# W2 in wider products and smaller pieces, another path for the second norm of two blocks, and a new written-out order in a transformer block on one core

## The chip, the core and the metric

The kernel runs on one core of a Trainium2 chip. The core has a matrix engine (TensorE: PE in the profile, PEld for its weight loads), a vector engine (DVE), an activation engine (ACT), GpSimd (POOL) and SyncE (SP), which here issues nearly all DMAs. The metric is the device time of one execution in microseconds. Three runs of the kernel before gave 1135.32, 1136.92 and 1138.43 us; the median is 1136.92.

## The reference

One block of a transformer with adaptive layer norm, on 2048 tokens of 1024 features in bf16. Attention has 32 heads of 32 features for the queries and a single head for keys and values; the feed-forward part is gated and has 3584 hidden features.

```
mod = silu(c) @ w_mod            # six vectors: sa, ca, ga, sb, cb, gb
h = layernorm(x) * (1 + ca) + sa
q = (h @ wq), 32 heads;  k = h @ wk;  v = h @ wv      # one k and one v for all heads
p = softmax(q k^T / sqrt(32))
x = x + ga * ((p v) @ wo)
h = layernorm(x) * (1 + cb) + sb
x = x + gb * ((silu(h @ w1) * (h @ w3)) @ w2)
```

## The kernel before

**Tiles.** The tokens are split into 8 blocks of 256 (`NB`, `B`), each of two tiles of 128 tokens (`t`). Within a block, attention goes over 8 groups of 4 heads (`f`), each group being a "unit" `u = 8n + f`, and over 8 steps `j` of 256 keys. One step `c` (`s_exp`) is 8 score products of 32 rows, which run four at a time in TensorE's row groups, followed by two exponentials on ACT of 128x1024 each, which are written to one of 10 slots of `U`. There are 512 steps, and so 1024 exponentials. The scores use six PSUM banks (`S` in the profile), everything else the other two (`PB`); after the last exponentials the six are used as well.

**Attention's sums.** The denominators are sums over keys: DVE adds pairs of exponentials (`pairs`, into `PS`), then folds these together (`fold`, and the additions in `av`), and TensorE multiplies what is left by ones (`dens`). `av_mm` multiplies the exponentials by V. `attend` transposes, inverts and multiplies, and writes the result over the queries in `QT`.

**After a block's attention.** `wo(n)` multiplies by WO, adds to `X`, takes the statistics of the second norm (`ln_stats`: two BATCH_NORM_STATS2 and an aggregate on DVE, an addition and a power on POOL) and normalises each tile to `XN` (`ln_norm`). The result must then be transposed into `h2t(n)`. In blocks 1 to 6 each tile is transposed by a DMA (DMA_TRANSPOSE), and DVE scales eight rows of 256 in place. In blocks 0 and 7 TensorE transposes through PSUM, in two halves of the features, each of which needs both tiles; DVE scales on the way out. `ffn1` then goes over 14 slabs of 256 hidden features (W1 and W3, 512 KB each, in three slots), with a tanh on ACT for each. `ffn2` multiplies by W2 in four quarters of 256 output columns: `quarter(n, q)` loads 1.8 MB (`w2_dma`, into one of two slots of `W2S`), and runs 28 products of 256 columns for each of the two tiles into the two halves of one bank; `result` scales by `GBR` and adds to `X`. In the last block the last two quarters' weights go to room in `QT` and `U` that is free by then.

**The start.** Sixteen tiles of x are loaded, normalised (`lnt1`: statistics on DVE; the normalising, `nm`, and the evacuation of the transposed tile, `ev`, on ACT or DVE), transposed on TensorE, and projected to K, V and Q. WQ is loaded in two parts. Its first 256 columns are scaled to `WQ0S` for the first heads; later DVE scales all of WQ in place, in eight instructions by row group, for the remaining query projections. `q_bias` makes the bias of the queries by 48 products of one column for six head groups. `mod_chunk` makes four of the modulation vectors from eight pieces of 1 MB.

**Order.** Every operation is a node of a graph with an engine, an estimated duration, a due time `vt` and a tag. `Placer.run` builds each engine's order from these ahead of time: it takes the node that can start first, and among those within a slack the one with the least `vt` plus an offset from `PLAN`. `PLAN` has one entry for each 8 steps of attention: slacks, flags and offsets by tag and engine. On the chip each engine runs its order strictly, with semaphore waits; an SP wait for a free slot holds every DMA behind it. TensorE's products may be emitted in a form of four 32-column products (`prods`, `cols`, profile "128\*32"), which avoids a switch of the array's mode next to V products but has four times the instructions; `mode_of` chooses this form while the run of such products is under `COLS` and an estimate of instruction traffic (`load`) is under `FULL`.

All engine instructions come out of one helper, so the profile gives line 22 for all of them; they are told apart by the tiles that they write and read.

## Time and profile before

| | |
|---|---|
| median of three runs | 1136.92 us |
| the profiled execution | 1139.48 us, of which the span is 1137.5 us |
| granted TensorE clock, mean | 0.992 |
| chain that ended last | PE 48%, ACT 42%, DVE 6% |
| DMA | 209.64 MB, 184 GB/s over the span |
| first exponential starts / last one ends | 30.8 us / 1038.1 us |

The page's first part gives busy time by engine, and the views of the trace group instructions by form ("out<-in", partitions x elements), list them in order of time, or say what ended an engine's idle time. `W2S` holds W2's slots (and, at the start, tiles of x and pieces of w_mod); `HT` holds the first norm's output and later the hidden features and `TS`; `W` is the W1/W3 slots and before that WQ; `WO` holds small things at the start. The idle time that is put down to "issue" is time in which an engine waited for nothing that the profile shows. The mean duration of a matmul includes its way through the array: the spacing of a run of them is shorter.

### The profile page before, as it was taken

How to read it: one execution, taken by the hardware profiler on the slowest of the kernel's cores; microseconds unless marked ns; L12 is line 12 of the kernel's file. 1: busy time of each engine (PE TensorE's matmuls, PEld its weight loads, DVE VectorE, ACT ScalarE, POOL GpSimd, SP SyncE). 2: the span in 40 equal slices, each digit the busy share in tenths (PEclk: the TensorE clock that was granted, in tenths of full speed). 3: DMA queues.
4: the chain of work that ended last, by engine and by line, in shares of the span. 5: the costliest groups of instructions: out<-in, count | busy, mean ns of one | idle time of the engine just before them, and what ended most of it. 6: DMA issues, size and time to landing. Idle time of an engine off the chain costs nothing.

```text
span 1137.5 us, 37371 instructions
## 1 busy us (share of the span) xinstructions
PE 1102.1 (97%) x16835; PEld 752.4 (66%) x16860; DVE 989.8 (87%) x1617; ACT 1020.1 (90%) x1159; POOL 39.1 (3%) x91
## 2 busy tenths in 40 slices
PE   5999998999899999999999999999999999999998
PEld 4744536766467766777577766776567757776887
DVE  7998999999989989998999899998989899997442
ACT  5999999999999999999999999999989999994110
POOL 5200000000000000000000000000000000000000
PEclk9999989999999999999999999999999999999999
DMA  9320586675756666865596577868686558767993
GB/s 347 104 76 22 166 217 187 193 205 139 168 150 194 190 176 160 240 190 151 137 287 192 151 190 202 227 193 216 142 245 192 156 152 226 210 198 197 239 240 103
DMA packets 381535, 209.64 MB, mean 184 GB/s; under 512 B 17600, under 2 KB 373184, under 8 KB 381376
## 3 DMA queue, kind: packets, MB, share of 16 engines
q1 hardware_dynamic: 380944, 207.11, 65.9%
q8 instruction: 133, 2.18, 0.8%
q14 instruction: 26, 0.21, 0.1%
q10 hardware_dynamic: 432, 0.13, 0.0%
HBM read 199.89 MB, written 4.19 MB: 179 GB/s over the span
## 4 chain that ended last, share of the span: by engine, by line
PE 48%; ACT 42%; DVE 6%; DMA 1%; issue 1%; SPq 1%; POOL 0%; DVEq 0%
ACT U L22 39%; PE PB L22 34%; PE S L22 14%; ACT HT L22 3%; DVE PS L22 2%; DMA W<-in_A_wq_dram 1%; DVE ST L22 1%; SPq L22 1%; DVE X L22 1%; DVE RB L22 0%; DVE QT L22 0%; DVE HT L22 0%; DVE XNB L22 0%; DVE WO L22 0%; DVE MV L22 0%
## 5 line engine op out<-in xcount | busy, mean ns | idle before, releaser
L22 ACT ACTIVATE U<-S 128x1024 bf16<-128x1024 f32 x1024 | 966.6, 1142 | 11.5 <-PE S L22 10.7
L22 DVE TENSOR_TENSOR PS<-U 128x2048 bf16<-128x2048 bf16 x256 | 308.2, 1216 | 12.0 <-ACT U L22 10.1
L22 DVE TENSOR_TENSOR PS<-PS 128x1024 bf16<-128x1024 bf16 (+1 forms) x420 | 282.5, 689 | 2.5
L22 PE MATMUL PB<-QT,W 128*128 128x256 bf16 (+1 forms) x2688 | 228.1, 276 | 0.4 <-DVE HT L22 0.4
L22 PE MATMUL S<-QT,KT 32*128 32x256 bf16 x4096 | 204.7, 274 | 10.1 <-ACT U L22 7.8
L22 PEld LDWEIGHTS PB<-QT,W 128*128 128x128 bf16 (+1 forms) x2688 | 171.2, 98 | 42.0 <-issue 23.6
L22 PE MATMUL PB<-W2S,HT 128*128 128x256 bf16 x1512 | 189.3, 273 | 0.0
L22 PEld LDWEIGHTS PB<-W2S,HT 128*128 128x128 bf16 x1512 | 137.4, 98 | 41.5 <-issue 22.0
L22 PEld LDWEIGHTS S<-QT,KT 32*128 32x128 bf16 x4096 | 60.8, 92 | 139.5 <-ACT U L22 130.9
L22 PE MATMUL PB<-U,V 128*32 128x256 bf16 x4096 | 130.9, 276 | 3.5 <-issue 2.3
L22 PEld LDWEIGHTS PB<-U,V 128*32 128x32 bf16 x4096 | 101.8, 97 | 27.8 <-issue 15.3
L22 PE MATMUL PB<-QT,HT 128*128 128x256 bf16 (+1 forms) x1216 | 117.0, 273 | 0.0
L22 PE MATMUL PB<-HT,W 128*32 128x512 bf16 (+2 forms) x884 | 99.2, 343 | 3.1 <-DVE XNB L22 1.0
L22 PEld LDWEIGHTS PB<-QT,HT 128*128 128x128 bf16 (+1 forms) x1216 | 86.4, 97 | 21.0 <-issue 11.4
L22 ACT ACTIVATE HT<-PB 128x512 bf16<-128x512 f32 (+1 forms) x105 | 77.0, 733 | 7.9 <-PE PB L22 7.8
L22 DVE SCALAR_TENSOR_TENSOR HT<-HT,PB 128x512 bf16<-128x512 bf16 x100 | 68.3, 683 | 6.7 <-ACT HT L22 6.5
L22 PEld LDWEIGHTS PB<-HT,W 128*128 128x128 bf16 (+1 forms) x896 | 50.6, 97 | 34.3 <-issue 13.4
L22 DVE TENSOR_TENSOR HT<-HT,PB 128x512 bf16<-128x512 bf16 x100 | 68.2, 682 | 4.4 <-PE PB L22 3.1
L22 ACT ACTIVATE HT<-S 128x512 bf16<-128x512 f32 (+1 forms) x17 | 12.1, 721 | 58.9 <-PE S L22 58.9
L22 DVE STREAM_TRANSPOSE RB<-PB 128x256 f32<-128x256 f32 x63 | 28.0, 444 | 33.8 <-PE PB L22 33.4
L22 PE MATMUL PB<-WO,QT 128*128 128x512 bf16 (+1 forms) x260 | 53.2, 381 | 1.4 <-issue 0.6
L22 POOL TENSOR_SCALAR RS<-MV 128x1 f32<-128x1 f32 x32 | 10.2, 322 | 1009.3 <-DVE MV L22 1008.6
(111 smaller groups left out, 661.7 us busy)
## 6 DMA issues: line engine op xcount, KB each, us to landing
W<-in_B_w_dram SPq DMA_DIRECT2D x150, 512.0 KB, 4.6
W2S<-in_B_w_dram SPq DMA_DIRECT2D x30, 1792.0 KB, 8.5
HT<-in_B_w_dram SPq DMA_DIRECT2D x74, 512.0 KB, 4.7
W2S<-in_w_mod_dram SPq DMA_DIRECT2D x8, 1024.0 KB, 6.3
X<-in_A_x_dram SPq DMA_DIRECT2D x8, 512.0 KB, 7.2
U<-in_w_mod_dram SPq DMA_DIRECT2D x4, 1024.0 KB, 12.2
out_dram<-X SPq DMA_DIRECT2D x7, 512.0 KB, 7.7
W2S<-in_A_x_dram SPq DMA_DIRECT2D x5, 512.0 KB, 9.7
```

The source lines that it names most:

```text
L22: return getattr(e, call[0])(*call[1], **call[2])
```

## The change

- **W2.** `half(n, h)` takes the place of `quarter`: two halves of 512 output columns, each in two passes (one for each tile of tokens) of 28 products of 512 columns, one bank for each pass. W2 is loaded in pieces of 7 x 128 hidden rows by 512 columns (0.9 MB), four for a half. The second pass goes through the pieces backwards, and the next half takes the slots in the order in which they come free. The result is scaled and added 512 columns at a time; in the last block there are three stores in place of five.
- **Second norm.** Block 1 now goes through TensorE like blocks 0 and 7, and all three do it tile by tile: eight transposes of one tile, then eight scalings of 128 columns. In these blocks the addition in `ln_stats` is on DVE in place of POOL.
- **The last unit of blocks 0 and 1** uses `av_sharp`: the last two steps' exponentials go into the denominators as products with ones, without DVE's additions, and six of the eight V steps no longer wait for the unit's last exponentials.
- **Start.** Tiles 3, 5 and 7 have their statistics on ACT (`act_stats`: two passes with accumulation, and four small POOL operations). WQ is scaled on POOL, by columns of one head group each, so that a projection waits for its own part alone. The query bias of six groups comes from 32 products of 192 columns and a transpose. The modulation pieces have earlier due times.
- **Order.** `load`, `FULL` and `FETCH` go. In their place the planner counts PE instructions in units of 256 (`fetched`), estimates when each block of them arrives from when it is asked for and from the DMA load, and delays PE's planned time until then. A switch from the 32-column form to scores costs 0.09 more. `PLAN` is new: nearly all entries differ.

The diff without `PLAN`, cut:

```diff
     SWITCH = {"F": 0.095, "S": 0.11, "A": 0.106, "C": 0.106}
+    CS = 0.09
...
-    FULL = 36.0
-    FETCH = 24.0
+    BLOCK, AHEAD, STOP, CALL, MOST, LAND = 256, 141, 430, 0.6, 4.5, 2.6
...
-        return n.col[1][0] or ("C" if self.mode in ("A", "C") and self.ncol < self.COLS and self.load < self.FULL else "F")
+        return n.col[1][0] or ("C" if self.mode in ("A", "C") and self.ncol < self.COLS else "F")
...
+    def fetched(self, count):
+        self.pos += 2 * count
+        while self.pos >= self.BLOCK * len(self.fetch) + self.AHEAD:
+            self.fetch.append(min(max(self.t["pe"] + self.CALL, self.bw), self.t["pe"] + self.CALL + self.MOST) + self.LAND)
+        while self.pos >= self.BLOCK * self.got + self.STOP:
+            self.t["pe"] = max(self.t["pe"], self.fetch[self.got])
+            self.got += 1
...
+        if near:
+            op("dve", lambda: [lambda e: e.tensor_scalar(RS[:, tt:tt + 1], MV[:, tt, 1:2], EPS, None, ALU.add)], 0.12,
+               reads=[("MV", tt)], writes=[("RS", tt)], vt=vt)
...
+    def act_stats(xap, tt, keys, vt):
+        op("act", lambda: [lambda e: e.activation(JUNK[:], xap, ACT.Copy, accum_out=AS[:, tt, 0:1])], 0.95, reads=keys,
+           writes=["JUNK", ("AS", tt)], vt=vt)
...
+        op("act", lambda: [lambda e: e.activation(JUNK[:], xap, ACT.Square, bias=NB_[:, tt:tt + 1],
+                                                  accum_out=AS[:, tt, 1:2])], 0.95, reads=keys + [("NB", tt)],
+           writes=["JUNK", ("AS", tt)], vt=vt)
...
-        ln_stats(xap, tt, xkey(tt), vt)
+        (act_stats if tt in ONACT else ln_stats)(xap, tt, xkey(tt), vt)
...
+    def q_bias_rest(vt):
...
+            BANK[b][32 * g:32 * (g + 1), 0:192], SABR[:, cc, 0:32],
+            WQ[:, cc, 2 * P:NC * P].rearrange("p (f q) -> p f q", q=P)[:, :, 32 * g:32 * (g + 1)], start=(cc == 0),
...
+    def av_sharp(u):
...
+        for q in range(0, NP - 2, 2):
+            pairs(c0 + q)
...
+            av_mm(u, c0 + q, q, s, q == 0, q == NJ - 1, [exps[(c0 + (5 if q < 6 else 7), 1)]])
...
+        terms = [("U", c0 + q, kk) for q in (6, 7) for kk in range(2)]
+        terms = [("PS", 0, 0), ("PS", 4, 0)] + terms
...
-            ln_stats(X1[:, n % NX, t, :], 2 * n + t, xk(n, t), vt)
+            ln_stats(X1[:, n % NX, t, :], 2 * n + t, xk(n, t), vt, n < 2 or n == NB - 1)
...
-            if 0 < n < NB - 1:
+            if 1 < n < NB - 1:
...
-        for hh in range(2):
+        for t in range(2):
             s = Sess()
...
+            op("pe", lambda b, t=t: [lambda e, cc=cc: e.transpose(
+                BANKH[b][:, cc * P:(cc + 1) * P], XN[t][:, cc * P:(cc + 1) * P], IDENT[:]) for cc in range(NC)], 0.5,
...
+            for cc in range(NC):
+                op("dve", lambda b, t=t, cc=cc: [lambda e: e.tensor_scalar(
+                    h2t(n)[:, cc, t * P:(t + 1) * P], BANKH[b][:, cc * P:(cc + 1) * P], MODC[:, 3, cc:cc + 1],
+                    MODC[:, 2, cc:cc + 1], ALU.mult, ALU.add)], 0.2,
...
+    def w2_slot(n, h, k):
+        if n == NB - 1 and h:
+            return W2X[k], ("W2X", k)
+        r = 3 - k if h else k
+        return W2P[r], ("W2P", r)
...
-    def quarter(n, q, vt):
+    def half(n, h, vt0, vt1):
         G.tag = "quarter"
...
+        for k in range(4):
+            w2_dma(n, h, k, vt0 + k - (200 if n == NB - 1 and h and k < 2 else 20))
...
+            order = [(k, i) for k in (range(4) if t == 0 else range(3, -1, -1)) for i in range(NK)]
...
+                    lambda e: e.matmul(BANK[b], HHT[:, f, t * P:(t + 1) * P], w2[:, i, :], start=first, stop=last)],
...
+    def result(n, h, t, vt, s):
...
+        op("dve", lambda b: [lambda e: e.tensor_tensor(o2, BANK[b], GBR[:, h * 512:(h + 1) * 512], ALU.mult)], 0.7,
...
+        op("dve", lambda: [lambda e: e.tensor_tensor(xs, xs, o2, ALU.add)], 0.34, reads=kr + k, writes=k, vt=vt)
...
-    q_bias(2, NC, "WQ1", -1400)
-    for cc in range(NC):
-        op("dve", lambda cc=cc: [lambda e: e.tensor_scalar(WQ[:, cc, :], WQ[:, cc, :], MODC[:, 1, cc:cc + 1], None,
-                                                           ALU.mult)], 0.43,
...
+    q_bias_rest(-1400)
...
+        op("pool", lambda f=f: [lambda e: e.tensor_tensor(
+            WQ[:, :, f * P:(f + 1) * P], WQ[:, :, f * P:(f + 1) * P],
+            MODC[:, 1, :].unsqueeze(2).broadcast_to([P, NC, P]), ALU.mult)], 2.3,
...
-        mod_chunk(i, 8.0 + 5 * i)
+        mod_chunk(i, 4.0 + 3 * i)
...
-            av(8 * n + f)
+            (av_sharp if f == NC - 1 and n < 2 else av)(8 * n + f)
```

More of the change, by code (lines that the diff above doesn't have):

```diff
@@ L254 @@
+    (0.1, 0.02, 0.29, 1, 3.3, {"av/pe": 1, "d11/sp": 21, "d8/sp": 1, "kb/pe": -22, "ln/pe": 6, "mc/pe": -5,
+     "pair/dve": 18, "q/pe": 1, "d2/sp": 0, "s/pe": 0}),
+    (0.1, 0.17, 0.29, 0, 2.6, {"av/dve": 88, "d11/sp": 23, "d2/sp": -4, "d4/sp": -8, "out/sp": -1, "q/pe": 9,
+     "quarter/pe": -5, "quarter/sp": 6, "slab/sp": -8, "v/pe": 25, "d6/sp": 0, "d8/sp": 0, "wo/sp": 0}),
 ]
@@ L285, in __init__ @@
         self.ncol = 0
-        self.load = 0.0
+        self.pos = 0
+        self.fetch = []
+        self.got = 0
         self.run_of = None
@@ L432, in commit @@
                 fn = n.col[0] if self.mode == "C" else fn
-            r = 9.2 if self.mode == "F" else 36.7 if n.col is None or dur < 0.3 else 18.4
-            self.load = max(0.0, max(0.0, self.load - self.FETCH * (start - before)) + (r - self.FETCH) * dur)
             if self.mode == "A":
@@ new lines, in half @@
+            result(n, h, t, vt, s)
+            if n == NB - 1 and (t or ends):
+                G.tag = "out"
+                t0 = t if ends else 0
+                k = [x for tx in range(t0, t + 1) for x in xk(n, tx, (2 * h, 2 * h + 1))]
+                outs.append(dma("sp", out2[n * B:(n + 1) * B, h * 512:(h + 1) * 512].rearrange(
+                    "(t p) d -> p t d", p=P)[:, t0:t + 1], X1[:, n % NX, t0:t + 1, h * 512:(h + 1) * 512],
+                    ("OUT", n, h, t), (t + 1 - t0) * P * 1024, reads=k, vt=vt))
+                G.tag = "quarter"
@@ L1225, in ffn2 @@
     def ffn2(n, vt0, vt1):
-        for q in range(4):
-            quarter(n, q, vt0 + (vt1 - vt0) * q / 4)
+        for h in range(2):
+            half(n, h, vt0 + (vt1 - vt0) * h / 2, vt0 + (vt1 - vt0) * (h + 1) / 2)
         if n == NB - 1:
```

461 lines of the change are left out of this document (260 added, 201 removed), and 4 rows, old and new, of the table PLAN.

## The prediction

> **What bounds the kernel now.** I read the page first, then busy time by stretch, then who ACT waited for, then the timeline around each place that the change touches.
>
> ```profile
> PE 1102.1 (97%) x16835; PEld 752.4 (66%) x16860; DVE 989.8 (87%) x1617; ACT 1020.1 (90%) x1159; POOL 39.1 (3%) x91
> ...
> L22 ACT ACTIVATE U<-S 128x1024 bf16<-128x1024 f32 x1024 | 966.6, 1142 | 11.5 <-PE S L22 10.7
> ```
>
> ```profile
> 30.80:1038.10 1007.30, 987.48 (x15670) 654.39 (x15693) 925.06 (x1485) 995.41 (x1128) 22.15 (x46) 0.99 0.65 177
> ...
> 0.00:30.80 30.80, 18.06 (x262) 15.14 (x263) 23.51 (x60) 16.32 (x19) 15.21 (x42) 1.00 0.98 349
> 1038.10:1137.50 99.40, 96.54 (x908) 82.85 (x906) 41.23 (x74) 8.36 (x14) 1.69 (x4) 1.00 0.78 205
> ```
>
> The page alone suggests PE. The stretches (length, then busy time and instructions of PE, PEld, DVE, ACT and POOL, the granted clock, the DMA engines' share and GB/s; cut at the first exponential, 30.8, and at the end of the last, 1038.1) say more. In the **head** the DMA engines are at 0.98 of their time. In the **body** ACT is busy for 995.4 of 1007.3 us: the exponentials set the pace, and everything that could be won there without taking work off ACT is 11.9 us. In the **tail** PE is busy for 96.5 of 99.4 us. So a PE saving in the body does not shorten the body; it is worth something only where it fills an ACT gap, or where it means that less work is left over for the tail.
>
> **The W2 products.** All 1792 products of 256 columns become 896 of 512, for the same columns.
>
> ```profile
> L22 PE MATMUL S<-W2S,HT 128*128 128x256 bf16 x168 | 19.2, 273 | 0.0
> ...
> L22 PE MATMUL S<-WO,QT 128*128 128x512 bf16 x31 | 6.9, 379 | 0.1
> ```
>
> ```profile
> 1035.78 3.23 PE L22 MATMUL PB<-W2S,HT 128*128 128x256 bf16 x28
> ...
> 1040.80 3.01 PE L22 MATMUL S<-W2S,HT 128*128 128x256 bf16 x26
> ...
> 1043.97 1.70 PE L22 MATMUL S<-W2S,HT 128*128 128x256 bf16 x14
> ...
> 1045.72 6.85 PE L22 MATMUL S<-WO,QT 128*128 128x512 bf16 x31
> ...
> 1052.41 1.91 PE L22 MATMUL S<-W2S,HT 128*128 128x256 bf16 x16
> ...
> 1054.16 3.66 PE L22 MATMUL PB<-W2S,HT 128*128 128x256 bf16 x32
> ...
> 1058.55 2.13 PE L22 MATMUL PB<-W2S,HT 128*128 128x256 bf16 x18
> ...
> 1117.72 6.28 PE L22 MATMUL S<-W2S,HT 128*128 128x256 bf16 x56
> ...
> 1134.73 0.42 DVE L22 TENSOR_TENSOR HT<-S,GBR 128x256 bf16<-128x256 f32 x1 [2.31 <-PE S L22]
> 1135.19 0.29 DVE L22 TENSOR_TENSOR X<-X,HT 128x256 bf16<-128x256 bf16 x1
> ```
>
> Spacing of 256 columns: (6.28 - 0.273)/55 = 0.1092 us. Of 512: (6.85 - 0.379)/30 = 0.2157. A pair becomes one for 2 x 0.1092 - 0.2157 = 0.0027 us less: 2.4 us over 896 pairs, 0.3 us of it in the last block's 112. The weight loads that go (896) lie under the matmuls and are worth nothing by themselves. At the very end the last result is now 512 columns wide in place of 256, so its two operations take up to twice the 0.42 + 0.29, and its store doubles as well: I take +0.4, no more than +0.7. That eats the 0.3.
>
> **What the tail can give.** The rows above show 28+26+14+16+32+18 = 134 W2 products of block 6 that PE still had when the exponentials ended, 14.6 us. They are not all waste: the last attention's sums (1040.80 to 1045.72) and the last norm (from 1052.41 until the 18 products at 1058.55 are through) leave PE nothing else; those fills are 40 and 66 products, 11.6 us. So with no backlog the tail would lose only about 28 x 0.109 = 3.1 us, unless those chains shorten too. The change shortens the second one: one POOL addition of a norm goes to DVE, and the first tile's transposes and scalings are done before the second is normalised, for about 1 to 2 us. Does the backlog shrink? PE's idle time is made in blocks 0 and 1:
>
> ```profile
> 172.25 1.07 POOL L22 TENSOR_SCALAR RS<-MV 128x1 f32<-128x1 f32 x1 [3.48 <-DVE MV L22]
> ...
> 174.61 1.07 PE L22 MATMUL PB<-IDENT,XNB 128*128 128x128 bf16 x16 [0.47 <-DVE XNB L22]
> ...
> 175.40 2.64 DVE L22 TENSOR_SCALAR HT<-PB,MODC 128x256 bf16<-128x256 bf16 x8
> ...
> 176.91 0.94 PE L22 MATMUL PB<-HT,W 128*128 128x256 bf16 x6 [0.90 <-DVE HT L22]
> ```
>
> ```profile
> 309.16 1.24 SPq L22 DMA_TRANSPOSE QT<-XNB  x1
> ...
> 316.22 2.13 DVE L22 TENSOR_SCALAR QT<-QT,MODC 128x256 bf16<-128x256 bf16 x8
> ...
> 317.83 1.70 PE L22 MATMUL PB<-QT,HT 128*128 128x256 bf16 x14
> ```
>
> In block 1 the normalised tile leaves for its transposing DMA at 309.16 and the first product that uses it comes at 317.8, after that DMA and other DVE work ahead of the scalings. Through TensorE this is 8 transposes (half of the 16 that took 1.07) and 8 scalings of 128 columns (between 0.2 and 0.33 each, 16 for two tiles; the row has 0.33 for 256), so products could start near 312.5: some 5 us of PE won, for about 1.1 us of PE transposes and up to 2.6 us of DVE added (16 x 0.3 for 8 x 0.27). In block 0 the by-tile order and the DVE addition (the POOL one took 1.07) win 1 to 2 us; the shorter last sums (fewer DVE additions, more products with ones) 1 to 3 us in each. With 2.1 us of W2 that is 9 to 14 us of PE before the tail, near the whole backlog. I take **-3.5 us** for the tail (bounds -6, all fills shortened, and +0.5, no backlog removed and the wider end).
>
> **What the body can give.** ACT's waits after 30 us, whole and for 800 to 900:
>
> ```profile
> ACT U L22 <- PE S L22: 10.7, 15, 2.2
> ...
> ACT U L22 <- PE S L22: 3.9, 4, 2.2
> ```
>
> ```profile
> 834.55 0.29 PE L22 MATMUL PB<-U,V 128*32 128x256 bf16 x4 [2.33 <-issue]
> ...
> 835.46 1.94 ACT L22 ACTIVATE U<-S 128x1024 bf16<-128x1024 f32 x2 [2.18 <-PE S L22]
> ```
>
> ```profile
> q8 instruction: 133, 2.18, 0.8%
> ```
>
> The largest wait is at 832: PE stands for 2.33 us with nothing that the profile shows holding it, in a run of 32-column products, each with its own weight load. 33,695 PE instructions over 133 instruction transfers are 253 in each, so a run of narrow products eats transfers fastest. The new order books such a transfer before it lays out the products, and W2 has 1792 instructions (7 transfers) fewer; it also drops the old limit on narrow products, so more of them may appear. I take -2.5 of the 3.9 us for this stall and what follows it, with 0 as the other bound, and -1.5 of the other 6.8 us of waits; a new order can also make waits, which I bound by +4. **-4 us.** That it was this fetch is an inference from "issue" and the count. The Trainium skill, "Runtime: NRT & Kernel Launch", section "Instruction fetch mechanics", says instructions stream in 16 KiB blocks of 256 and the fetch is mostly hidden. The block size agrees with the 253; by "hidden" the planned fetches would win nothing, and the sum would be 2.5 us poorer.
>
> **The head.** Statistics of three tiles go to ACT (two passes each, 1.27 us for a pass like it), the scaling of WQ from DVE to POOL.
>
> ```profile
> 24.22 1.71 DVE L22 TENSOR_SCALAR WO<-W,MODC 128x256 bf16<-128x256 bf16 x6 [0.41 <-DMA W<-in_A_wq_dram]
> 24.28 2.03 POOL L22 TENSOR_SCALAR WO<-W,MODC 128x256 bf16<-128x256 bf16 x2 [1.68 <-DMA W<-in_A_wq_dram]
> ...
> 30.31 0.40 PE L22 MATMUL S<-QT,KT 32*128 32x256 bf16 x8
> ```
>
> ```profile
> L22 DVE BATCH_NORM_STATS2 ST<-W2S 128x6 f32<-128x512 bf16 x20 | 12.8, 666 | 1.0 <-DMA W2S<-in_A_x_dram 1.0
> ...
> L22 ACT ACTIVATE XNB<-W2S,NB,RS 128x1024 bf16<-128x1024 bf16 x3 | 3.8, 1266 | 0.1
> ...
> L22 DVE TENSOR_SCALAR W<-W,MODC 128x1024 bf16<-128x1024 bf16 x8 | 3.8, 473 | 0.0
> ...
> L22 POOL COPY WO<-SAB 128x1024 bf16<-128x1024 bf16 x1 | 1.0, 1037 | 2.1 <-DVE SAB L22 2.1
> ```
>
> WQ's first piece lands at 24.2 and its place in the queue hardly moves, so the first exponential can't come much before 28; the 6 us from 24.2 to the scores at 30.31 are scaling, product, eviction and some queueing. DVE is relieved of 3 x 2 x 0.67 + 3.8 = 7.8 us, ACT takes 6 x 1.27 = 7.6 us, and had 14.5 us free before 30.8. I take **-0.5 us** (bounds -2.5 and +3, if these passes delay ACT's evictions). POOL's 8 scalings lie between 1.04 us each (the copy) and 4.1 (four times 1.02, the 256-column row), nearer the second in kind; they hide under the exponentials of the first heads, since WQ's part for head group 2 is used tens of us later.
>
> **Sum:** -3.5 - 4 - 0.5 = -8 us on the profiled execution's 1139.5 (span 1137.5 and 2.0 around it), so 1131.5 there. That execution was 2.6 above the median of the three runs, 1136.9, so the forecast is **1129 us**; its own range is 1122 to 1133.
>
> **The rivals.** *Nothing to measure* (1135 to 1137): ACT keeps its pace, the waits move elsewhere, and the backlog only turns into idle PE. For it: the 11.9 us is a hard ceiling, and 11.6 of the 14.6 us were useful fill. Against it: 1131 needs no more than a third of what is idle.
>
> *W2 pieces come late* (slower, about 1143).
>
> ```profile
> W2S<-in_B_w_dram SPq DMA_DIRECT2D x30, 1792.0 KB, 8.5
> HT<-in_B_w_dram SPq DMA_DIRECT2D x74, 512.0 KB, 4.7
> ```
>
> ```profile
> 895.97 1.48 PE L22 MATMUL PB<-W2S,HT 128*128 128x256 bf16 x12
> ...
> 947.02 1.05 PE L22 MATMUL PB<-W2S,HT 128*128 128x256 bf16 x8
> ```
>
> W2 of a block takes 52 us, a pass of 28 rows 13 us. Before, a freed slot had 13 us for 1.8 MB (8.5 us). Now the second half's pieces take the slots that the second pass frees: 9.75 us for 0.9 MB, which is 4.7 to 8.5 us by the rows. It holds while the queue is clear; it decides from a landing over 9.75 us. Then PE waits in order, scores stand behind it, and SP holds the next loads too. With 2 us a block passed on to ACT in 7 blocks: +14 - 8 = +6. Against it: bytes per us are the same, and the slots are freed in the order of need.
>
> *POOL holds DVE up* (about 1140): eight POOL operations of up to 4.1 us are 33 us between 35 and 75. DVE has 8% free (it is busy for 925 of the body's 1007 us), some 3 us of those 40, plus the 7.8 it is relieved of; past 1.4 us held per operation it delays the exponentials' buffers, at 2.7 us by 11, which leaves +3. The rows at 24.2 speak against it: six DVE scalings ran in 1.71 us beside POOL's. The Trainium skill, "SBUF — State Buffer", section "SBUF: two separate sides", has this rule: the two share a port pair as an exclusive lock, and the loser blocks for a whole instruction. By it in full the time would be up to 14 us worse than now (33 - 11 - 8); the rows at 24.2 don't bear that out.
>
> **The numbers.** Forecast 0.60, nothing 0.18 (0.03 of it just faster), late pieces 0.15 (0.02 of it the same), POOL 0.07 (0.02 the same). About 0.3%, 3.4 us, can be told from no change here: faster 0.63, same 0.19, slower 0.18. The range goes from the best bounds of the sum with little left out, 1121, to near the late pieces, 1142.
>
> **What would show it.** Right: ACT busy over 99% between first and last exponential, no "issue" wait of PE above 1 us, block 1's first slab products within 5 us of its norm, a tail below 97 us. Wrong: PE waiting for DMA before W2 products, longer DVE operations while POOL scales WQ, or new ACT gaps in the first 60 us.

## The result and the profile after

The kernel after takes 1153.48 us in the median of four runs (1150.93 to 1153.97), the kernel before on the same chip 1136.13 us (1135.32 to 1138.43): a ratio of 1.0145, 95% interval 1.0123 to 1.0167 (the ratios here are estimated over all executions of a set; the two medians alone give 1.0153). The change makes the kernel slower by some 17 us where 8 us less were forecast.

The traces hold 11.6 us of these 17: the profiled execution of after is the fastest of its four (1150.93 us, span 1149.1), that of before was above its median (1139.48 us, span 1137.5). The granted clock differs a little too: 0.991 in this execution of after and 0.987 to 0.990 in its other three, 0.992 in the profiled one of before. What share of the rest that is was not separated (see the last section).

The page of after, two lines of its parts 1 and 5, and then the stretches head, body and tail, cut as for before at the first exponential (29.07) and at the end of the last (1050.97); columns as before: length, busy time and instructions of PE, PEld, DVE, ACT and POOL, clock, DMA share, GB/s.

```profile
PE 1100.8 (96%) x14441; PEld 666.2 (58%) x14512; DVE 997.7 (87%) x1626; ACT 1024.6 (89%) x1168; POOL 60.8 (5%) x98
...
L22 ACT ACTIVATE U<-S 128x1024 bf16<-128x1024 f32 x1024 | 966.6, 1144 | 19.6 <-PE S L22 13.5
```

```profile
0.00:29.07 29.07, 18.94 (x277) 16.04 (x278) 19.67 (x49) 17.44 (x24) 15.41 (x42) 1.00 0.98 347
29.07:1050.97 1021.90, 990.45 (x13457) 586.43 (x13521) 935.67 (x1497) 998.79 (x1130) 44.27 (x55) 0.99 0.60 177
1050.97:1149.10 98.13, 91.44 (x708) 63.72 (x713) 42.36 (x81) 8.36 (x14) 1.10 (x2) 1.00 0.67 187
```

PE has 2394 matmuls fewer (16835 before) and is busy for 1.3 us less; POOL is busy for 60.8 us in place of 39.1. Head 1.7 us shorter, tail 1.3 us shorter, body 14.6 us longer (1021.9 for 1007.3); ACT's idle time in the body has grown from 11.9 to 23.1 us. Where in the body is told by the start times of single exponentials, counted from 0 (us, from the traces' records of the exponentials):

| exponential | before | after | difference |
|---|---|---|---|
| 0 | 30.79 | 29.07 | -1.72 |
| 16 | 49.86 | 51.58 | +1.72 |
| 24 | 57.80 | 68.32 | +10.52 |
| 64 | 94.93 | 105.64 | +10.71 |
| 512 | 533.25 | 542.77 | +9.52 |
| 832 | 848.90 | 857.96 | +9.06 |
| 1023 | 1036.94 | 1049.75 | +12.81 |

So 12.2 us are lost between exponentials 0 and 24, 8.8 of them in the 17 us from 51.6 to 68.3. From exponential 64 on, in some 940 us, another 2.1 are lost. DVE's instructions of after in that place, in order of time (start, duration, instruction; in brackets, where an engine was idle, the idle time before it and what ended it):

```profile
50.87 2.71 DVE L22 TENSOR_TENSOR PS<-U 128x2048 bf16<-128x2048 bf16 x1
53.50 0.28 DVE L22 TENSOR_TENSOR V<-PB,VBR 128x128 bf16<-128x128 f32 x1
53.70 2.71 DVE L22 TENSOR_TENSOR PS<-PS 128x2048 bf16<-128x2048 bf16 x1
56.34 2.91 DVE L22 TENSOR_TENSOR PS<-U 128x2048 bf16<-128x2048 bf16 x1
59.17 0.28 DVE L22 TENSOR_TENSOR V<-PB,VBR 128x128 bf16<-128x128 f32 x1
59.37 3.97 DVE L22 TENSOR_TENSOR PS<-PS 128x2048 bf16<-128x2048 bf16 x2
63.26 0.28 DVE L22 TENSOR_TENSOR V<-PB,VBR 128x128 bf16<-128x128 f32 x1
63.46 1.22 DVE L22 TENSOR_TENSOR PS<-U 128x2048 bf16<-128x2048 bf16 x1
```

POOL's in the same place, and the group they belong to:

```profile
48.57 12.43 POOL L22 TENSOR_TENSOR W<-W,MODC 128x1024 bf16<-128x1024 bf16 x5
```

```profile
L22 POOL TENSOR_TENSOR W<-W,MODC 128x1024 bf16<-128x1024 bf16 x8 | 18.3, 2305 | 0.2 <-DVE QBI L22 0.2
```

While POOL scales WQ (48.57 to 61.00), DVE's additions, 1.22 us each otherwise, take 2.7 to 2.9 (of the two in the row of 59.37 the first takes 2.71, the second 1.23); from 63.46 on, with POOL done, they take 1.22 again. The evictions of V beside them, which read PSUM, stay at 0.28. Four additions lose 6.2 us in this way and three normalisings 2.5 (last section), 8.7 us of DVE in all. What that does to the exponentials is in the rows of PE and of ACT:

```profile
53.84 1.04 PE L22 MATMUL PB<-WO,HT 128*128 128x32 bf16 x32 [1.66 <-DVE V L22]
...
59.51 0.99 PE L22 MATMUL PB<-WO,HT 128*128 128x32 bf16 x32 [2.43 <-DVE V L22]
60.43 0.62 PE L22 MATMUL S<-QT,KT 32*128 32x256 bf16 x8
```

```profile
61.64 1.94 ACT L22 ACTIVATE U<-S 128x1024 bf16<-128x1024 f32 x2 [3.14 <-PE PB L22]
66.10 1.94 ACT L22 ACTIVATE U<-S 128x1024 bf16<-128x1024 f32 x2 [2.52 <-PE S L22]
```

The eviction of V stands in DVE's queue behind a stretched addition; PE waits for it 2.43 us; the scores stand behind that product in PE's order (60.43), and ACT gets nothing for 3.14 us. A short operation that isn't stretched itself is late all the same, because of its place in the queue.

The tail of after, PE in order of time from the end of the last exponential to the first slab of the last block:

```profile
1053.11 1.89 PE L22 MATMUL PB<-W2S,HT 128*128 128x512 bf16 x8 [0.16 <-issue]
1054.84 2.32 PE L22 MATMUL S<-W2S,HT 128*128 128x512 bf16 x10
1057.09 0.29 PE L22 MATMUL S<-PS,ONES 128*32 128x256 bf16 x4
1057.31 1.68 PE L22 MATMUL S<-W2S,HT 128*128 128x512 bf16 x7
1058.83 7.07 PE L22 MATMUL S<-WO,QT 128*128 128x512 bf16 x31
1065.74 1.67 PE L22 MATMUL S<-W2S,HT 128*128 128x512 bf16 x7
1067.25 0.61 PE L22 MATMUL PB<-IDENT,XNB 128*128 128x128 bf16 x8
1067.70 1.03 PE L22 MATMUL S<-W2S,HT 128*128 128x512 bf16 x4
1070.68 0.62 PE L22 MATMUL PB<-IDENT,XNB 128*128 128x128 bf16 x8 [1.96 <-DVE XNB L22]
1072.13 4.00 PE L22 MATMUL S<-QT,HT 128*128 128x256 bf16 x32 [0.83 <-DVE QT L22]
```

The backlog of W2 is 8+10+7+7+4 = 36 products of 512 columns, 7.8 us. Before had 134 of 256 by the prediction's rows, 14.6 us; but 21 of the 28 in the row of 1035.78 started before the last exponential ended (1038.05), so that 113, 12.3 us, are the like number. The backlog is smaller by 4.5 us, but PE now stands idle in the norm (1.96 and 0.83 us) where the backlog filled it.

### The profile page after: what moved, and what is told of

Its sections match the earlier page's. It is cut to its first block, busy times and chain, and to the rows that moved or that the text cites. A ratio compares the mean times of both kernels' runs of the same rounds, so it can differ in the third digit from the quotient of the medians.

```text
span 1149.1 us, 32698 instructions
## 1 busy us (share of the span) xinstructions
PE 1100.8 (96%) x14441; PEld 666.2 (58%) x14512; DVE 997.7 (87%) x1626; ACT 1024.6 (89%) x1168; POOL 60.8 (5%) x98
## 4 chain that ended last, share of the span: by engine, by line
PE 62%; ACT 24%; DVE 9%; DMA 1%; issue 1%; POOL 1%; SPq 1%
PE PB L22 47%; ACT U L22 23%; PE S L22 15%; DVE PS L22 3%; DVE QT L22 1%; DVE ST L22 1%; DMA W<-in_A_wq_dram 1%; ACT HT L22 1%; POOL RS L22 1%; DVE HT L22 1%; DVE X L22 1%; DVE XNB L22 1%; SPq L22 1%; DVE WO L22 0%; DVE RB L22 0%
## 5 line engine op out<-in xcount | busy, mean ns | idle before, releaser
L22 ACT ACTIVATE U<-S 128x1024 bf16<-128x1024 f32 x1024 | 966.6, 1144 | 19.6 <-PE S L22 13.5
L22 DVE TENSOR_TENSOR PS<-PS 128x1024 bf16<-128x1024 bf16 (+1 forms) x415 | 286.3, 699 | 3.0
L22 PE MATMUL PB<-QT,W 128*128 128x256 bf16 (+1 forms) x1904 | 231.6, 273 | 0.7
L22 PE MATMUL PB<-W2S,HT 128*128 128x512 bf16 x737 | 184.2, 380 | 5.0 <-issue 4.1
L22 PE MATMUL PB<-QT,HT 128*128 128x256 bf16 (+1 forms) x941 | 121.0, 275 | 0.4
L22 PEld LDWEIGHTS PB<-W2S,HT 128*128 128x128 bf16 x784 | 66.4, 97 | 86.3 <-issue 21.7
L22 PEld LDWEIGHTS PB<-QT,HT 128*128 128x128 bf16 x942 | 86.5, 98 | 25.2 <-issue 10.5
L22 PE MATMUL PB<-HT,W 128*128 128x256 bf16 (+1 forms) x546 | 97.4, 321 | 2.3 <-issue 1.9
L22 DVE TENSOR_TENSOR HT<-HT,PB 128x512 bf16<-128x512 bf16 x104 | 71.1, 684 | 6.3 <-PE PB L22 4.7
L22 PEld LDWEIGHTS PB<-HT,W 128*128 128x128 bf16 x560 | 49.9, 99 | 36.6 <-issue 12.1
L22 PE MATMUL PB<-WO,QT 128*128 128x512 bf16 x217 | 55.0, 380 | 1.8 <-issue 0.8
L22 POOL TENSOR_SCALAR RS<-MV 128x1 f32<-128x1 f32 x23 | 12.3, 534 | 624.8 <-DVE MV L22 624.0
```

Of the source, the lines that this page charges most:

```text
L22: return getattr(e, call[0])(*call[1], **call[2])
```

## The experiments

The theory (A): POOL's scaling of WQ, an operation with two tensor inputs, keeps DVE from its additions, and DVE has no slack there. The rivals: another part of the change costs the time (late pieces of W2, the wider products, the order), or the scalings' own work and the projections' wait for it do. In all runs but two (6 and 7) every engine keeps the order of the kernel that was edited, apart from the operations that a run adds or moves. The kernel before was timed beside each set on the same chip: 1138.03 (first four), 1138.59 (next four) and 1136.84 us (last three).

**1. The scalings made small.** POOL's eight operations keep their places, but cover 2 columns of each 128, so that most of WQ stays unscaled.

```diff
-            WQ[:, :, f * P:(f + 1) * P], WQ[:, :, f * P:(f + 1) * P],
-            MODC[:, 1, :].unsqueeze(2).broadcast_to([P, NC, P]), ALU.mult)], 2.3,
+            WQ[:, :, f * P:f * P + 2], WQ[:, :, f * P:f * P + 2],
+            MODC[:, 1, :].unsqueeze(2).broadcast_to([P, NC, 2]), ALU.mult)], 2.3,
```

> The changed kernel with every engine's order and waits kept; each of POOL's eight scalings of WQ now covers 2 columns of each group of 128 (16 elements a partition in place of 1024), so the rest of WQ stays unscaled. Theory A (POOL's scalings hold DVE's operations on SBUF, which delays the exponentials by some 9 to 11 us between the 16th and the 24th): DVE's pair additions take 1.22 us there again instead of 2.7, the 64th exponential starts about 9 to 11 us earlier, at 95 to 97, and the median falls from 1153.5 to about 1143. Theory B (the new order of the first 70 us is slow by itself, with statistics on ACT and V late; POOL's scalings are bystanders): within 2 us of 1153.5, the 64th exponential at 104 to 106.

Measured: 1141.12 us (1139.19 to 1146.09), ratio 1.0028 (1.0014 to 1.0041), close to what theory A expects. The additions between 34 and 75 us, by form:

```profile
L22 DVE TENSOR_TENSOR PS<-U 128x2048 bf16<-128x2048 bf16 x10 | 12.1, 1214 | 1.7 <-ACT U L22 1.7
...
L22 DVE TENSOR_TENSOR PS<-PS 128x2048 bf16<-128x2048 bf16 x4 | 4.9, 1213 | 0.0
```

They are back at 1.21 us, and exponential 64 starts at 94.86, 0.07 us before that of the kernel before. At this size the eight operations leave 0.28% of the 1.45%: the rest of the change costs 1.6 to 4.7 us, even with DVE rid of WQ.

**2. The scalings alone.** The kernel before, with the eight operations added behind DVE's own scaling; their result goes to `GBR`, which is overwritten later.

```diff
+    for f in range(8):
+        op("pool", lambda f=f: [lambda e: e.tensor_tensor(
+            GBR[:].rearrange("p (c f) -> p c f", c=NC), WQ[:, :, f * P:(f + 1) * P],
+            MODC[:, 1, :].unsqueeze(2).broadcast_to([P, NC, P]), ALU.mult)], 0.01,
+            reads=["WQ0", "WQ1", ("MODC", 1)], writes=[("GBR", 0), ("GBR", 1)], vt=-1100 + f)
```

> The kernel before, every engine's order kept, with eight extra multiplications on POOL of the same form (128x8x128 by a broadcast) that read the scaled WQ and write GBR before it is used; nothing waits for them except GBR's later writer. Theory A: DVE's additions take 2 to 3 us while they run (about 48 to 67 us), the exponentials after that are 6 to 11 us later, the time is 1142 to 1147. Theory B: no change, 1135 to 1138.

Measured: 1148.81 us (1147.86 to 1151.73), ratio 1.0093 (1.0076 to 1.0109): 10.8 us more, a little above the range of theory A, for work that nobody waits for. That also speaks against the rival that the projections' wait for the scalings is what costs: here no projection waits for them. Groups between 34 and 75 us in this run, then the same groups before:

```profile
L22 DVE TENSOR_TENSOR PS<-U 128x2048 bf16<-128x2048 bf16 x7 | 15.2, 2176 | 0.0
...
L22 DVE TENSOR_TENSOR PS<-PS 128x2048 bf16<-128x2048 bf16 x4 | 8.6, 2153 | 0.0
```

```profile
L22 DVE TENSOR_TENSOR PS<-U 128x2048 bf16<-128x2048 bf16 x9 | 10.9, 1216 | 0.1
...
L22 DVE TENSOR_TENSOR PS<-PS 128x2048 bf16<-128x2048 bf16 x4 | 4.9, 1214 | 0.0
```

The stretch is 7 x 0.96 + 4 x 0.94 = 10.5 us, and exponential 64 is 10.35 us late: us for us. The single records show how it comes about: eight additions are stretched, and each ends 1.08 us after the end of a POOL operation that had begun before it.

**3. The same scaling in one-input form, in small pieces.** The kernel after; each scaling is eight POOL TENSOR_SCALARs of 128 columns.

```diff
-        op("pool", lambda f=f: [lambda e: e.tensor_tensor(
-            WQ[:, :, f * P:(f + 1) * P], WQ[:, :, f * P:(f + 1) * P],
-            MODC[:, 1, :].unsqueeze(2).broadcast_to([P, NC, P]), ALU.mult)], 2.3,
+        op("pool", lambda f=f: [lambda e, c=c: e.tensor_scalar(
+            WQ[:, c, f * P:(f + 1) * P], WQ[:, c, f * P:(f + 1) * P], MODC[:, 1, c:c + 1], None, ALU.mult)
+            for c in range(NC)], 2.3,
```

> The changed kernel, orders kept, correct result; each scaling on POOL is now eight instructions of 128 columns by a per-partition factor in place of one of 8x128. Theory A, held for one whole instruction: DVE waits for a shorter piece each time, so an operation loses at most 0.3 to 0.5 us, and more than half of the 10.9 us comes back (1143 to 1148). If it is POOL's total time that counts, or if eight small ones take longer than one, nothing comes back or it gets worse (1153 to 1165). Theory B: 1153.

Measured: 1156.5 us (1153.45 to 1157.23), ratio 1.0148 (1.0131 to 1.0166), no better than after. By the time alone the theory would have fallen. The groups of DVE between 34 and 75 us and of POOL say why it does not:

```profile
L22 DVE TENSOR_TENSOR PS<-U 128x2048 bf16<-128x2048 bf16 x7 | 8.6, 1236 | 1.7 <-ACT U L22 1.7
L22 DVE TENSOR_TENSOR PS<-PS 128x2048 bf16<-128x2048 bf16 x4 | 5.0, 1250 | 0.0
```

```profile
L22 POOL TENSOR_SCALAR W<-W,MODC 128x128 bf16<-128x128 bf16 x64 | 49.3, 789 | 0.3 <-DVE QBI L22 0.3
```

```profile
56.35 0.58 DVE L22 TENSOR_SCALAR XNB<-W2S,MV,RS 128x1024 bf16<-128x1024 bf16 x1 [4.26 <-POOL NB L22]
```

The additions are no longer stretched. But 64 operations take 0.79 us each, 49 us in place of 18, and the norms' small POOL operations stand in the queue behind them: DVE waits 4.26 us for one, and 8.8 us in five such waits between 30 and 107 us (after has none). One cost has taken the place of the other. It left open whether the form or the shortness of the operations sets DVE free; runs 5, 10 and 11 are about that.

**4. W2 in products of 256 again.** The kernel after; each product of 512 is issued as two of 256, in the places that the planner gave it.

```diff
+        if n.tag == "quarter" and e == "pe":
+            calls = [(c[0], (c[1][0][:, z:z + 256], c[1][1], c[1][2][:, z:z + 256]),
+                      {"start": c[2]["start"] and z == 0, "stop": c[2]["stop"], "skip_group_check": True})
+                     for c in calls for z in (0, 256)]
```

> The changed kernel, planned orders kept, with every W2 product of 512 columns emitted as two of 256 with the same weights (1792 products again, pieces and passes as changed). By the prediction's term (0.0027 us a pair, 2.4 us of PE, mostly not on the path that sets the end) and 1792 more PE instructions: 0 to 4 us slower than the changed kernel, 1153 to 1158. If the wide products themselves are what costs in the W2 stretches (waits between weights and product), it is faster, 1148 to 1152.

Measured: 1155.5 us (1154.24 to 1155.97), ratio 1.0141 (1.0124 to 1.0158) beside 1.0145 of after. The width makes no difference that can be measured, neither for the loss nor as a gain.

**5. One-input operations of full length.** The kernel before with eight added POOL TENSOR_SCALARs of whole rows.

```diff
+        op("pool", lambda cc=cc: [lambda e: e.tensor_scalar(GBR[:], WQ[:, cc, :], MODC[:, 1, cc:cc + 1], None, ALU.mult)],
+           0.01, reads=["WQ0", "WQ1", ("MODC", 1)], writes=[("GBR", 0), ("GBR", 1)], vt=-1100 + cc)
```

> The kernel before, all orders kept, with eight extra POOL TENSOR_SCALARs of 1024 columns (one tensor input in place of the two of the run with extra TENSOR_TENSORs); their result is written to GBR and overwritten later. Theory, first form (what holds DVE up is a POOL operation with two tensor inputs): DVE's additions PS<-U and PS<-PS between 34 and 75 us stay at 1.22 to 1.3 us, exponential 64 within 1 us of before, time 1136 to 1141. Second form (any POOL operation that reads this memory holds DVE for its whole length, and the row-wise run escaped only because its operations were short): by the 256-column row (1.02 us) each takes some 4 us, the additions beside them 3 us or more, exponential 64 is 8 to 18 us late, time 1147 to 1157.

Measured: 1141.12 us (1138.57 to 1143.05), ratio 1.0021 (1.0009 to 1.0032). POOL's group, and the additions between 34 and 75 us:

```profile
L22 POOL TENSOR_SCALAR GBR<-W,MODC 128x1024 bf16<-128x1024 bf16 x8 | 26.9, 3357 | 4.3 <-DVE W L22 3.7
```

```profile
L22 DVE TENSOR_TENSOR PS<-U 128x2048 bf16<-128x2048 bf16 x8 | 12.6, 1581 | 0.1
L22 DVE TENSOR_TENSOR PS<-PS 128x2048 bf16<-128x2048 bf16 x4 | 4.8, 1210 | 0.0
```

Neither form of the expectation was right in full. Each operation is longer than a TENSOR_TENSOR (3.36 us for 2.76), but the stretch is 8 x 0.36 = 2.9 us in place of 10.5, and exponential 64 is 3.55 us late in place of 10.35. An operation of this form does hold DVE, but for about 0.4 us in the mean, not for its length. By the single records, five of the twelve additions beside POOL are held (1.47 to 2.02 us) and seven are not (1.21 to 1.22), and each held one ends 0.65 to 0.68 us before the POOL operation beside it does.

**6 and 7. WQ on DVE as before, and the POOL scalings spread over the first block, with a new order.** In run 6 the eight scalings are DVE's TENSOR_SCALARs of whole rows, as in the kernel before. In run 7 each POOL scaling but the first waits for a later exponential:

```diff
+    for k, w in enumerate(spread):
+        if k:
+            G._edge(exps[(6 + 8 * k, 0)], w, True)
```

> The kernel after with WQ scaled as before by eight DVE TENSOR_SCALARs of 1024 columns (one instruction per row group, so that all projections wait for all of WQ); the order is planned anew. POOL theory: the additions between 34 and 75 us are back at 1.22 us, DVE does 3.8 us more, time 1138 to 1146. Rival (another part of the change costs the time, and the smaller POOL operations helped by something else): 1149 or more.

> The kernel after with the eight POOL scalings of WQ spread out: each but the first waits for an exponential 8 steps after the one before (some 15 us apart, from 45 to 160 us), still ahead of the projection that needs it; the order is planned anew. Theory (what costs is that the scalings stand back to back and DVE has no slack to catch up): one or two additions of each 15 us take 2 to 2.9 us, the others 1.22, DVE's 8% of free time takes most of it, exponential 64 starts at 95 to 98 us, time 1139 to 1145. Rival (each scaling costs the pace what it holds DVE for, wherever it stands): exponential 128 still some 10 us late, time 1149 to 1155.

Measured: 1233.27 and 1231.39 us, ratios 1.0829 (1.0815 to 1.0844) and 1.0812 (1.0796 to 1.0827). These two tell nothing of POOL. Their order is planned anew from the entries of `PLAN` that belong to another graph, and the loss grows along the whole body (run 6: +11.5 us at exponential 64, +26.9 at 128, +52.6 at 512, +83.2 at 1023). Exponentials 16 to 24 take 8.1 us in run 7, as before (7.9; after 16.7), but that is one stretch of a kernel that is off everywhere. What they do show is how much the written-out offsets are worth: a graph that differs in eight operations loses 95 us with them. Whatever changes the edges or the planned durations can't be tried here without a new plan, so the parts of the change other than the scalings and the width were not tried one by one.

**8. The same scalings on DVE, in the same places.** The kernel after; the planner books POOL as before, but the instruction is issued on DVE.

```diff
-            self.emit(n, e, fn)
+            self.emit(n, "dve" if n.tag == "ws" else e, fn)
```

> The kernel after with all orders kept; the same eight scalings (TENSOR_TENSOR W<-W,MODC 128x1024), at the same places of the plan, are issued on DVE in place of POOL. By the row of PS<-PS 128x1024 (0.68 us) and twice that, each takes 0.7 to 1.4 us on DVE: 6 to 11 us more DVE work between 41 and 70 us, but no operation of DVE is stretched. POOL theory: additions at 1.22 us, exponential 64 2 to 8 us late, time 1143 to 1150, below the kernel after: on POOL the scalings cost DVE more than doing them itself. Rival (the loss is the scalings' own work or the projections' wait for it): 1151 or more.

Measured: 1151.27 us (1149.46 to 1153.38), ratio 1.0111 (1.0095 to 1.0127). Between 34 and 75 us:

```profile
L22 DVE TENSOR_TENSOR PS<-U 128x2048 bf16<-128x2048 bf16 x8 | 9.7, 1220 | 1.1 <-ACT U L22 1.1
L22 DVE TENSOR_TENSOR W<-W,MODC 128x1024 bf16<-128x1024 bf16 x7 | 8.5, 1215 | 0.0
L22 DVE TENSOR_TENSOR PS<-PS 128x2048 bf16<-128x2048 bf16 x4 | 4.9, 1219 | 0.0
```

DVE does the scalings in 1.22 us each (POOL took 2.31) and no addition is stretched. Exponential 64 is 8.8 us late for 8 x 1.22 = 9.7 us of work (one of the eight lies ahead of the first exponential), and with POOL 10.7 late. Both the delay (2 to 8 us were expected) and the time miss the theory's range, and the time lies in the rival's. By the time alone this run can't tell the two apart, because on DVE the scalings' own work costs nearly as much; run 2, where nobody waits for the result, can. DVE held by POOL costs a little more here than DVE needs for the same operations, and these are dear on either: in the old form, by rows, DVE needed 3.8 us for all of WQ.

**9. Fewer us on DVE.** As run 8, but the six head groups 2 to 7 are scaled in eight TENSOR_SCALARs of 768 columns at the place of the first of them; groups 0 and 1 stay TENSOR_TENSORs.

```diff
+                return [lambda e, c=c: e.tensor_scalar(WQ[:, c, 2 * P:], WQ[:, c, 2 * P:], MODC[:, 1, c:c + 1], None, ALU.mult)
+                        for c in range(NC)]
```

> The kernel after with all orders kept and POOL freed of WQ: the scalings of head groups 0 and 1 (TENSOR_TENSOR, 1.22 us each by the run before) and, at the place of group 2, eight TENSOR_SCALARs of 768 columns for the other six groups (the 1024-column form took 0.47, so some 0.37 each) are issued on DVE: 5.4 us of DVE in place of the 9.7 us of the run with all eight as TENSOR_TENSORs. Theory (the loss is the time for which DVE is kept from its additions, whoever keeps it, us for us): exponential 64 starts 3 to 5.5 us after that of before, time 1143 to 1147. Rival (the loss has a threshold, and 5 us of DVE go into its idle time): exponential 64 within 1.5 us, time 1139 to 1142.

Measured: 1147.36 us (1146.1 to 1147.57), ratio 1.0086 (1.007 to 1.0102). The group of eight took 2.7 us; with the other two (1.2 each) that is 5.1 us of DVE, and exponential 64 is 4.8 us late, as the theory has it. So 5 us of DVE do not go into its idle time: no threshold shows. The time is just above the range; what run 1 leaves may be the reason. This is the fastest of the versions of after that scale all of WQ, and it is still 10.5 us above the kernel before.

**10 and 11. Two inputs, or the pattern.** The kernel before with eight added POOL operations: in run 10 TENSOR_TENSORs of plain rows (the same row as both inputs), in run 11 TENSOR_SCALARs in the change's pattern of eight pieces of 128.

```diff
+        op("pool", lambda cc=cc: [lambda e: e.tensor_tensor(GBR[:], WQ[:, cc, :], WQ[:, cc, :], ALU.mult)],
...
```

```diff
+        op("pool", lambda cc=cc: [lambda e: e.tensor_scalar(
+            GBR[:].rearrange("p (c f) -> p c f", c=NC), WQ[:, :, cc * P:(cc + 1) * P], MODC[:, 1, cc:cc + 1], None, ALU.mult)],
...
```

> The kernel before, all orders kept, with eight extra POOL TENSOR_TENSORs whose two inputs are both plain rows of 1024 columns of WQ (nothing broadcast, no pattern of eight pieces); the result goes to GBR and is overwritten later. Theory (two tensor inputs are what holds DVE): the additions between 49 and 72 us take 2 us or more in the mean, exponential 64 8 to 12 us late, time 1146 to 1151. Rival (the broadcast or the pattern of eight pieces of 128 is what holds it): additions below 1.7 us in the mean, exponential 64 no more than 4.5 us late, time 1138 to 1143.

> The kernel before, all orders kept, with eight extra POOL TENSOR_SCALARs that read WQ in the pattern of the change (eight pieces of 128 columns), one tensor input. Theory (two tensor inputs are what holds DVE): as the run with extra TENSOR_SCALARs of whole rows, additions at 1.4 to 1.7 us in the mean, exponential 64 no more than 4.5 us late, time 1138 to 1143. Rival (the pattern): additions 2 us or more, exponential 64 8 to 12 us late, time 1146 to 1151.

Measured: 1149.85 us (1148.57 to 1150.77), ratio 1.0112 (1.0091 to 1.0134), and 1139.91 us (1137.08 to 1142.39), ratio 1.0025 (1.0013 to 1.0037). The additions between 34 and 75 us of run 10, then of run 11:

```profile
L22 DVE TENSOR_TENSOR PS<-U 128x2048 bf16<-128x2048 bf16 x7 | 15.2, 2174 | 0.0
L22 DVE TENSOR_TENSOR PS<-PS 128x2048 bf16<-128x2048 bf16 x4 | 8.6, 2154 | 0.0
```

```profile
L22 DVE TENSOR_TENSOR PS<-U 128x2048 bf16<-128x2048 bf16 x8 | 12.7, 1582 | 0.1
L22 DVE TENSOR_TENSOR PS<-PS 128x2048 bf16<-128x2048 bf16 x4 | 4.8, 1209 | 0.0
```

Run 10 repeats run 2, run 11 repeats run 5. It is the form with two tensor inputs that makes the difference, not the broadcast and not the pattern. Whether it is the second input itself or something else in which a TENSOR_TENSOR differs from a TENSOR_SCALAR was not separated.

DVE time taken away ahead of exponential 64, against the delay of that exponential to before. For runs 8 and 9 the work is what they add to run 1, whose exponential 64 is 0.07 us ahead of before:

| run | DVE time lost | exponential 64 |
|---|---|---|
| 2, two inputs with broadcast | 10.5 stretch | +10.35 |
| 10, two plain inputs | 10.5 stretch | +10.60 |
| 5, one input, rows | 2.9 stretch | +3.55 |
| 11, one input, pattern | 2.9 stretch | +2.59 |
| 8, scaled on DVE | 9.7 work | +8.77 |
| 9, rows on DVE | 5.1 work | +4.81 |

The two agree within about 1 us, but in one direction alone. In run 1 DVE has the 3.8 us of WQ less to do than before, and exponential 64 gains 0.07. ACT explains it: in before the 48 exponentials from 16 to 64 take 45.07 us, 0.94 each, and ACT is busy for 0.94 us with each of the 1024 (966.6 in all). Time taken from DVE is lost here, and time given to it is not won.

## Why the prediction was wrong

**The step that failed** is the last sentence on the head: "POOL's 8 scalings lie between 1.04 us each (the copy) and 4.1 (four times 1.02, the 256-column row), nearer the second in kind; they hide under the exponentials of the first heads". They took 2.3 us each, inside those bounds, and nothing waits long for their results. But they are not hidden from DVE, and in place of nothing the price was 10.8 us by exponential 64 (105.64 in after, 94.86 in run 1). The cover that the sentence names is time on another engine, while what they use up is DVE's.

**The evidence behind it was a row of another form.** The rival with the right mechanism was there ("POOL holds DVE up") with a chance of 0.07, and it was set low by one argument: "The rows at 24.2 speak against it: six DVE scalings ran in 1.71 us beside POOL's." That row is about TENSOR_SCALARs, with one tensor input, on both engines. Runs 5 and 11 show that POOL's operations of this form hold DVE for little, runs 2 and 10 that those of the change's form hold it for long. And the row had no unhindered time beside it: singly, its six scalings take 0.27 to 0.50 us, three of them 0.41 or more, while in after, at the same place with one POOL operation in place of two, six of seven take 0.27 to 0.29. Even this row held some half a microsecond of stretch. The threshold in the rival was wrong as well: "DVE has 8% free", and "past 1.4 us held per operation". Runs 8 and 9 show next to no slack: 9.7 us of DVE cost 8.8, and 5.1 cost 4.8. The 8% are a mean over the body, while the additions of the first units stood back to back (0.1 us of idle time ahead of nine of them in the row of before under run 2).

**The rule.** The Trainium skill, "SBUF — State Buffer", section "SBUF: two separate sides", counts DVE operations with two inputs in SBUF among those that contend, only against a GpSimd operation that reads SBUF, and says that the one that starts first holds the pair for its whole instruction. The prediction weighed this rule and took the row instead. The trace of after agrees with it for the change's form: additions at 2.7 to 2.9 us for 1.22, each of which ends 1.08 us after the scaling beside it, and evictions from PSUM unchanged at 0.28. The price "up to 14 us worse" was nearer than the forecast, with some luck: it took 4.1 us for an operation where 2.3 were measured, and took off 11 us of free DVE time that was not there. For one tensor input on POOL the runs don't bear out "whole instruction": additions that were held ended 0.65 us or more before the POOL operation did (run 5).

**The body's gain (-4) came to +2.1 after exponential 64.** One part of the term came true. The stall at 832 us went, and from exponential 768 to 832 after wins 3.2 us on before (+12.23 to +9.06); the largest wait of PE put down to "issue" is now 0.3 us, though many small ones have come. PE's row of the waits before, then of after:

```profile
PE PB L22 <- issue: 3.8, 10, 2.3
```

```profile
PE PB L22 <- issue: 6.8, 42, 0.3
```

The stall goes with the order of the kernel before, though not always: at the same product that kernel's PE order has a wait of 1.7 us in runs 2 and 11, 2.0 in run 10 and 0.4 in run 5, where 3.5 us came back between the same two exponentials. In the runs with the order of after no "issue" wait of PE in the body is longer than 0.5 us. That the planned fetches did this is not shown; the whole order is new.

What failed is the rest of the term: the 1.5 us of other waits that were to go, and the waits of a new order, which the sum had at nothing (its bound was +4). After loses 1.5 us from exponential 64 to 768 and 3.8 from 832 to 1023. The second loss, 3.8 to 3.9 us, is in all six traces with the order of after; the runs with the order of before lose 0.1 at most there. ACT's waits of after from 845 to 1050 us are

```profile
ACT U L22 <- PE PB L22: 1.9, 1, 1.9
ACT U L22 <- PE S L22: 1.5, 2, 1.0
ACT HT L22 <- PE PB L22: 1.4, 2, 1.2
```

or 4.8 us; before, from 849 to 1038, ACT waits 1.0 us for its exponentials' scores. In block 1 PE's gap did close, as forecast: it is idle for 1.0 us from 310 to 360 where it was for 6.4 from 300 to 350. ACT had stood idle for only 1.2 us there, so little of that could reach the time.

**The tail's gain (-3.5) came to -1.3.** The backlog did shrink by 4.5 us, the norm's chain did get shorter (from the W2 products behind WO's to the first slab 6.4 us, before 8.1), and the last slabs and W2 take 77.0 us in both. The size that was wrong is the part of the backlog that is no fill. The prediction put it at 28 products, 3.1 us; 21 of them had started before the last exponential ended, so 7 were left, 0.8 us. The rest was useful fill, as the prediction said, and PE now idles for 6.7 of the tail's 98.1 us (98.13 less 91.44) where it idled for 2.9. That the W2 work which moved out of the tail is what costs the 3.8 us from exponential 832 on is likely, since PE was already busy for over 99% of that stretch (200.99 of 201.48 us in before, from 835 to 1037); no run shows it.

**The head's gain (-0.5) came to -1.7.** It lies within the bounds of that step; what the statistics on ACT cost or won there by themselves no run shows.

**W2's pieces came in time.** No wait of PE for the DMA of W2 appears in the trace of after, and the pieces of 0.9 MB land in 6.8 us, below the 9.75 from which that rival was to decide:

```profile
W2S<-in_B_w_dram SPq DMA_DIRECT2D x60, 896.0 KB, 6.8
```

That rival was refuted by the trace, as argued. The prediction's gain from the width, 2.4 us in all, lies below what run 4 can see.

**Of the signs that the prediction named for being wrong**, two came: longer DVE operations while POOL scales WQ, and new ACT gaps (the first, of 3.14 us, ends at 61.64, just past the 60 us that it named).

**Still open:** which of the remaining parts costs the 1.6 to 4.7 us that run 1 leaves. Its trace (of the slowest of the twelve executions) is 0.1 us ahead of before at exponential 64 and 5.4 behind at 1023, 3.8 of it lost from 832 on, so the time lies in the new order of the later blocks; its parts could not be undone without a new plan.

## What to carry to other kernels

In this kernel, work moved from DVE to POOL was not moved off DVE, since POOL's operations and DVE's additions both take two tensor inputs from SBUF. Price such a move at the stretch of the DVE operations beside it, and look for a row of the same form, not only of the same engines. Slack is read where the work lands (idle time ahead of the instructions of that stretch), not from an engine's share over the span. A short operation on the critical path is late by whatever stands ahead of it in its engine's order, so a stretch of unimportant work behind which it queues costs in full.

## What the runs showed of the hardware

- **The longer POOL operation held DVE for less.** Eight POOL operations of 1024 columns: with two tensor inputs (TENSOR_TENSOR) 2.76 us each and 10.5 us of stretch on DVE, with one (TENSOR_SCALAR) 3.36 us each and 2.9 us of stretch (runs 2, 10 against 5, 11). Beside the first, all eight stretched additions end 1.08 us after a POOL operation's end, in run 2 as in run 10; beside the second, held additions end before it.
- **POOL is held as well.** A scaling takes 1.9 us where no addition or normalising is beside it (after, from 26.87), 2.9 between two stretched additions (from 52.46).
- **DVE's normalising, with one input from SBUF, is held too; a statistics pass was not.** In after, beside one POOL scaling (35.63 to 37.70), the statistics that start at 35.87 keep their 0.67 us, and the normalising that follows takes 1.51 us, where the one before it, which started ahead of the scaling, took 0.55. The two other normalisings that start during a scaling take 1.80 us (from 43.94) and 0.73 (from 50.01); all three end 0.28 us after the scaling beside them does.

```profile
35.63 2.07 POOL L22 TENSOR_TENSOR W<-W,MODC 128x1024 bf16<-128x1024 bf16 x1
```

```profile
35.40 0.55 DVE L22 TENSOR_SCALAR WO<-W2S,MV,RS 128x1024 bf16<-128x1024 bf16 x1
35.87 0.67 DVE L22 BATCH_NORM_STATS2 ST<-W2S 128x6 f32<-128x512 bf16 x1
36.47 1.51 DVE L22 TENSOR_SCALAR XNB<-W2S,MV,RS 128x1024 bf16<-128x1024 bf16 x1
```

- **POOL's time does not go in proportion to the columns.** Where DVE did not hold it, a TENSOR_SCALAR of 128 columns took 0.60 us and one of 1024 columns 2.85: eight times the work for 4.7 times the time (single records of runs 3 and 5; the means with waiting are 0.79 and 3.36).
- **A run's time goes with the granted TensorE clock.** In the 12 executions of run 1 the mean granted clock went from 0.990 to 0.998 and the time from 1146.09 down to 1139.19 us; a line through them falls by 0.76 us for each 0.001. In the 17 executions of the kernel before that were timed beside it (0.991 to 0.995) the line falls by 0.63, with more scatter. So a difference of a few us between two executions of one kernel can go with the clock; which of the two is the cause was not tested.
